# A conv and low-rank mixer on one core: earlier loads of two batches, a held transpose, and copies in one go

## The chip, the cores and the metric

The kernel runs on one core of a Trainium2 chip. The metric is the device time of one execution in microseconds; the time of a kernel is the median of several runs.

## The reference

Two layers follow one another. The first is a causal convolution over 7 taps, with one set of softmax weights for each of 8 heads of 24 channels. The second mixes along the sequence with a low-rank product, adds that to its input, and applies a two-layer network over channels, again with a residual.

```python
# x: (8, 4224, 192), weight: (8, 7); U: (4224, 32), V: (32, 4224), w_ch1: (192, 768), w_ch2: (768, 192)
w = softmax(weight, axis=-1)
y[b, s, head h] = sum over k of w[h, k] * x_padded[b, s + k, head h]   # 6 zeros ahead of x
xt = y.transpose(0, 2, 1)
h = xt @ U @ V
u = y + h.transpose(0, 2, 1)
ch = np.maximum(u @ w_ch1, 0.0) @ w_ch2
out = (u + ch).astype(np.float32)
```

## The kernel before

The 8 x 4224 rows are 264 tiles of 128 rows, 33 in a batch, and 8 tiles make a group: 33 groups in all, numbered 0 to 32. Groups are not aligned with batches: batch 0 is groups 0 to 3 and the first tile of group 4, and so on.

What is done for a batch:

- x is loaded from DRAM in four pieces (`x_part`, L76, by POOL's DMA queue, cast to bf16 on the way; the list of pieces is `XP`, L84). Pieces 0 and 1 go to the lower 64 partitions, 2 and 3 to the upper. Each batch has a tile of a pool of two (`xs`), so batch 2 takes over the memory of batch 0, and batch 3 that of batch 1. `x_zero` clears the 64 rows ahead of a batch.
- The convolution is a matmul with band matrices. Batches 0 and 1 use `conv` (L351), which reads x as loaded. Batches 2 to 7 use `conv32` (L317), which reads x and a copy shifted by 32 rows (`xb_sb`, one buffer) as well. POOL makes the copy in six steps (`x_shift`, L282, returns them as a list): two whole parts (L289, 2.74 us each, and L291, 0.50), then four that copy 32 partitions (L301, 2.74 or 3.08 us each). The result, `y_sb`, is evicted from PSUM by ACT and DVE.
- `tt` is the product with U: 33 matmuls (`tt_mm`, L391), a split into two bf16 halves (`tt_split`, L407), and a sum over four row blocks (`tt_sum`, L420: two matmuls at L423, then a cast by DVE at L417 to `tt_sb`).

What is done for a group:

- h: `h_group` (L483) multiplies `tt_sb` by V (8 matmuls at L452), and DVE adds the result to y (L474), which makes u. `transp` (L491) then has SP issue a DMA transpose of u into `uT`. Groups 0 and 1 are transposed on PE instead.
- W1: `w1` (L537), 36 matmuls at L549, with ReLU by ACT (L563) or DVE (L565). It returns the last matmul of each of its six column blocks (`ends`).
- W2: `w2` (L570), two tiles at a time: 12 matmuls at L576, an addition of u by DVE (L584), and a store that SP issues (L592).

Every engine runs its instructions in the order of the program, which is written out by hand. SP has the transposes and the stores in one row; POOL has the loads of x and the copies in one row. The order after the start is in `SLOTS` (L605). A slot names groups for W1, groups for W2, and work to be put ahead of a given pair of W2, each word a letter and numbers: `h4` is h of group 4 with its transpose, `t2` and `s2` are tt and its sum for batch 2, `c2:0:3` is conv of 3 heads of batch 2 from head 0, `d1` is conv of batch 1, `x2:4` asks for the copies of batch 2 and issues the first four steps. The steps left over are issued one after each load of the next batch, or after the W1 of a following slot.

Loads of later batches are placed by `LOADS` (L655). For each piece it names a group and a column block of its W1, and `held` (L594) makes the load wait until the last matmul of that block has run. Batch 2 has its two first pieces held to the end of W1 of group 1, and the other two to blocks 2 and 5 of W1 of group 2. The main loop (L769) goes through the slots: W1 first with the loads, then W2 pair by pair.

Of the kernel before, what the change touches and what calls it, by code (L numbers as in the profile page):

```python
# [14 lines left out]
def kernel(  # L15
# [10 lines left out]
    nc = tc.nc  # L26
# [29 lines left out]
    def bank():  # L56
        return psp.tile([P, 512], F32, name="ps", tag="ps")
# [12 lines left out]
    def x_tile(b):  # L70
        xt[b] = xs.tile([P, NB1 + 1, D], BF16, name="x_sb")

    def x_zero(b, eng):
        eng.memzero(xt[b][0:HB, 0, :])

    def x_part(b, r, s0, s1):  # L76

        blk = NB0 * r + s0 - 1
        return nc.gpsimd.dma_start(  # L79
            out=xt[b][HB * r : HB * r + HB, s0:s1, :],  # L80
            in_=x[b, blk * HB : (blk + s1 - s0) * HB, :].rearrange("(j p) d -> p j d", p=HB),
        )

    XP = [(0, 1, 17), (0, 17, NB0 + 1), (1, 0, 18), (1, 18, NB1 + 1)]  # L84
# [171 lines left out]
    def u_layout(up):  # L256
        nb = [nfull + (1 if 32 * jj < nlast else 0) for jj in range(4)]
        for a in range(4):
            for jj in range(4):
                nc.tensor.matmul(  # L260
                    out=up[jj][:, 0 : nb[jj] * R],
                    lhsT=Eq[32 * jj : 32 * jj + 32, a, :],
                    rhs=Ur[32 * jj : 32 * jj + 32, 0 : nb[jj], a * R : (a + 1) * R],
                    start=(a == 0),
                    stop=(a == 3),
                    tile_position=(32 * jj, 0),
                )
        for jj in range(4):
            evac(
                "AD"[jj % 2],  # L270
                U_sb[:, 0 : nb[jj], jj, :],
                up[jj][:, 0 : nb[jj] * R].rearrange("p (k r) -> p k r", r=R),
            )
# [77 lines left out]
    def conv(b, h0, nh, rs, engs, k0=0, k1=NT, pp=None):  # L351

        if yt[b] is None:
            yt[b] = ys.tile([P, NT, D], BF16, name="y_sb")
        nk = {r: min(k1, (NB0, NB1)[r] // 2) - k0 for r in rs}
        if pp is None:
            pp = {r: bank() for r in rs}
        w = nh * GS
        for hh in range(nh):
            h = h0 + hh  # L360
            for halo in range(2):
                for r in rs:
                    for c in range(2):
                        st = 1 - halo + c + 2 * k0
                        nc.tensor.matmul(  # L365
                            out=pp[r][HB * c : HB * c + HB, 0 : nk[r] * w].rearrange(
                                "p (k a) -> p k a", a=w
                            )[:, :, hh * GS : hh * GS + GS],
                            lhsT=bands[h // HQ][
                                HB * r : HB * r + HB, h % HQ, HB * halo : HB * halo + HB  # L370
                            ],
                            rhs=xt[b][
                                HB * r : HB * r + HB,
                                st : st + 2 * nk[r] - 1 : 2,
                                h * GS : h * GS + GS,
                            ],
                            start=(halo == 0),
                            stop=(halo == 1),
                            tile_position=(HB * r, HB * c),
                        )  # L380
        for n, r in enumerate(rs):
            j0 = NB0 // 2 * r + k0
            evac(
                engs[n % len(engs)],
                yt[b][:, j0 : j0 + nk[r], h0 * GS : h0 * GS + w],
                pp[r][:, 0 : nk[r] * w].rearrange("p (k a) -> p k a", a=w),
            )

    ttb = [[] for _ in range(B)]

# [99 lines left out]

    def transp(g):  # L491
        uTt[g] = uts.tile([P, 4, 3, P], BF16, name="uT")
        nc.sync.dma_start_transpose(
            out=uTt[g][:].rearrange("p i c t -> p (i c) t"),
            in_=ut[g][:].rearrange("p i c f k -> p (i c f k)"),
        )
# [70 lines left out]

    out_t = out.rearrange("b s d -> (b s) d").rearrange("(t p) d -> p t d", p=P)

    def w2(g, t0, n):  # L570

        hf, i = t0 // 4, t0 % 4
        cps = bank()
        for a in range(n):
            for m in range(MC):
                nc.tensor.matmul(  # L576
                    out=cps[:, a * D : (a + 1) * D],
                    lhsT=rlt[g][:, m, hf, (i + a) * P : (i + a + 1) * P],
                    rhs=W2_sb[:, m, :],
                    start=(m == 0),  # L580
                    stop=(m == MC - 1),
                )
        o = outs.tile([P, 2, D], F32, name="out_sb")
        nc.vector.tensor_tensor(  # L584
            out=o[:, 0:n, :].rearrange("p n (c k) -> p n c k", c=3),
            in0=cps[:, 0 : n * D].rearrange("p (n c k) -> p n c k", n=n, c=3),
            in1=ut[g][:, i : i + n, :, hf, :],
            op=ALU.add,
        )
        t = g * GT + t0  # L590
        eng = nc.scalar if t + n == NTT else nc.sync
        eng.dma_start(out=out_t[:, t : t + n, :], in_=o[:, 0:n, :])  # L592

    def held(ins, after):  # L594
        tc.add_manual_dep(
            ins.ins,
            after.ins.name,
            mybir.DependencyInfo(mybir.DependencyClass.Sync, mybir.DependencyReason.DATA),
            reason="load held back",
        )  # L600

    SLOTS = [  # L605
        ([0], [], {}),
        ([1], [0], {0: ["h0"], 1: ["h3"]}),
        ([2], [1], {0: ["d1", "h1"], 1: ["t1"], 3: ["s1"], 4: ["h4", "x2:4"]}),
        ([3], [2], {1: ["h5"], 3: ["h6"]}),
        (  # L610
            [4, 5],
# [2 lines left out]
                0: ["h7"],  # L614
                2: ["c2:0:3:AAD"],
                3: ["c2:3:3:AAD"],
                4: ["c2:6:2:A", "x3:3"],
                6: ["t2"],
                8: ["s2", "h8"],
                10: ["h9"],  # L620
            },
        ),
    ]
# [1 line left out]
    for k in range(5, 14):  # L625
# [13 lines left out]
        elif k < 10:  # L639
            b = k - 2  # L640
# [11 lines left out]
        SLOTS.append((gs, gs, {p: [w for w in what if w] for p, what in at.items()}))  # L652
    assert nh == NG

    LOADS = {2: [(1, 5), (1, 5), (2, 2), (2, 5)], 3: [(4, 1), (4, 4), (5, 1), (5, 4)]}  # L655
    for b in range(4, B):
        g = 3 * b - 6
        LOADS[b] = [(g, 0), (g, 3), (g + 1, 0), (g + 1, 3)]

# [21 lines left out]
        conv(0, h, 2, [0, 1], "AA" if h == 0 else "AD", *KP[0][1:])  # L681
    work = [bank() for _ in range(4)]
    u_layout(work)
    o = 0
    for js in late:
        nc.gpsimd.tensor_copy(
# [42 lines left out]
    yT_part(1, parts1)  # L729
    hT_part(1, parts1)  # L730
    band2 = cst.tile([P, H, QB], BF16, name="band2")
    x_tile(1)
    x_zero(1, nc.gpsimd)
    for xp in XP:
        x_part(1, *xp)
    for r in range(4):
        q = slice(QB * r, QB * r + QB)
# [6 lines left out]
    def do(what):  # L744
        if what[0] == "c":
            b, h0, n, engs = what[1:].split(":")
            conv32(int(b), int(h0), int(n), engs)
            return
        if what[0] == "d":
            for h in range(H):  # L750
                conv(int(what[1:]), h, 1, [0, 1], "AD")
            return
        if what[0] == "x":
            b, n = (int(v) for v in what[1:].split(":"))
            steps.extend(x_shift(b))
            for _ in range(n):
                steps.pop(0)()
            return
        n = int(what[1:])
        if what[0] == "h":  # L760
            h_group(n)
            if n > 1:
                transp(n)
        elif what[0] == "t":
            tt_split(n, tt_mm(n, range(NT)))
        else:
            tt_sum(n)

    for gs1, gs2, at in SLOTS:  # L769
        for g in gs1:  # L770
            ends = w1(g, RELU0 if g == 1 else RELU)
            for b, blocks in LOADS.items():
                for q, (gb, m) in enumerate(blocks):
                    if gb == g:
                        if q == 0:
                            x_tile(b)
                            x_zero(b, nc.gpsimd)
                        held(x_part(b, *XP[q]), ends[m])
                        if steps:
                            steps.pop(0)()  # L780
            if g == 0:
                do("h2")
        while steps and gs1 != [3]:
            steps.pop(0)()
        npc = 4 * len(gs2)
        for p in range(npc + 1):
            for what in at.get(p, []):
                do(what)
            if p < npc:
                g, k = gs2[p // 4], p % 4  # L790
                if g == NG - 1 and k == 3:
                    w2(g, 6, 1)
                    w2(g, 7, 1)
                else:
                    w2(g, 2 * k, 2)
# [30 lines left out]
```

## Time and profile before

| what | value |
|---|---|
| median of 5 runs | 328.16 us (327.48 to 328.97) |
| the profiled execution | 329.81 us |
| its span, from first to last instruction | 328.0 us |
| PE busy | 319.6 us, 97% |
| DVE busy | 270.0 us, 82% |
| ACT busy | 170.1 us, 52% |
| POOL busy | 143.6 us, 44% |
| moved by DMA | 53.52 MB, mean 163 GB/s |
| median from issue to landing: transposes of u | 4.4 us |
| the same, pieces of x (384 KB) | 8.7 us |

The engines are PE (matmuls, with PEld loading weights beside it), DVE, ACT, POOL and SP. Times are microseconds from the start of the span unless they are marked otherwise. A line of the timeline has the start, the length, the engine, the line of code, the operation, the tile written and the tile read, and a count; in brackets at its end stands how long the engine was idle before it and what ended that. The chain of waits follows the work that ended last back from the end of the span, at each step to what released it. Queue q0 of the DMA is POOL's, with the loads; q1 is SP's, with transposes and stores. The ends of matmuls are modelled, so two rows of PE may overlap. The DMA bytes of a load of x count what is written (bf16).

### The profile page before, as it was taken

Reading aid. Unit: us, or ns where it says so; the run is one execution under the profiler, and the core shown is the slowest. Engines: PE = TensorE matmul, PEld = TensorE weight load, DVE = VectorE, ACT = ScalarE, POOL = GpSimd, SP = SyncE. Lnnn points to the kernel's source line nnn. Section 1 sums busy time; section 2 is a strip of 40 time slices with the busy share of each in tenths; the row PEclk is TensorE's granted clock in tenths of the full one; section 3 lists DMA queues with packets and bytes.
Section 4 is the critical chain, followed back from the end, with each engine's and each line's share of the span. In section 5 each row is a group of like instructions: output and inputs, shape, how many; then the busy total and the mean of one; then the engine's idle time right before and its main releaser. Section 6 shows DMA issues by size and latency. Waiting matters only on the chain.

```text
span 328.0 us, 9592 instructions
## 1 busy us (share of the span) xinstructions
PE 319.6 (97%) x3998; PEld 221.5 (68%) x3998; DVE 270.0 (82%) x552; ACT 170.1 (52%) x343; POOL 143.6 (44%) x112
## 2 busy tenths in 40 slices
PE   8999999999999999999999999999999999999994
PEld 3666576577557746866874784587797497497494
DVE  7659999987877987898798799879888898896853
ACT  1667524761666198068429708834903903903900
POOL 8493229834993895967669498000000000000000
PEclk9999999999999999999999999999999999999999
DMA  9999994999999999699989967039269069049034
GB/s 105 193 132 185 200 241 111 126 192 218 252 154 185 197 188 187 180 173 168 193 236 126 221 175 195 27 107 249 59 169 265 3 153 282 2 142 244 2 129 161
DMA packets 122907, 53.52 MB, mean 163 GB/s; under 512 B 87760, under 2 KB 122832, under 8 KB 122864
## 3 DMA queue, kind: packets, MB, share of 16 engines
q1 hardware_dynamic: 84528, 38.08, 49.0%
q0 software_dynamic: 38192, 14.73, 40.3%
q8 instruction: 31, 0.51, 0.6%
q14 instruction: 12, 0.10, 0.1%
q10 hardware_dynamic: 144, 0.10, 0.1%
HBM read 29.49 MB, written 25.95 MB: 169 GB/s over the span
## 4 chain that ended last, share of the span: by engine, by line
PE 81%; POOL 8%; DMA 6%; DVE 3%; issue 1%; POOLq 0%
PE ps L576 36%; PE ps L549 32%; POOL xb_sb L301 5%; DMA x_sb<-in_x_dram 4%; PE ps L335 3%; PE ps L155 3%; PE ps L452 3%; DMA uT<-u_sb 2%; PE ps L397 2%; POOL x_sb L79 1%; PE ps L365 1%; DVE rl_sb L565 1%; DVE y_sb L254 1%; POOL xb_sb L289 1%; DVE u_sb L474 1%
## 5 line engine op out<-in xcount | busy, mean ns | idle before, releaser
L563 ACT ACTIVATE rl_sb<-ps 128x512 bf16<-128x512 f32 x233 | 124.3, 604 | 109.6 <-PE ps L549 89.3
L576 PE MATMUL ps<-W_sb,rl_sb 128*128 128x192 bf16 x1584 | 141.9, 246 | 0.2
L576 PEld LDWEIGHTS <-rl_sb 128*128 128x128 bf16 x1584 | 128.0, 98 | 13.8 <-issue 13.2
L549 PE MATMUL ps<-uT,W_sb 64*128 64x512 bf16 x1188 | 131.6, 376 | 0.6 <-DMA uT<-u_sb 0.5
L565 DVE TENSOR_SCALAR rl_sb<-ps 128x512 bf16<-128x512 f32 x163 | 105.6, 687 | 16.6 <-PE ps L549 16.4
L549 PEld LDWEIGHTS <-W_sb 64*128 64x128 bf16 x1188 | 64.0, 94 | 63.8 <-issue 3.5
L584 DVE TENSOR_TENSOR out_sb<-ps,u_sb 128x384 f32<-128x384 f32 (+1 forms) x133 | 70.3, 548 | 25.9 <-PE ps L576 25.3
L301 POOL COPY xb_sb<-x_sb 32x3072 bf16<-32x3072 bf16 (+1 forms) x24 | 67.6, 2824 | 0.7
L474 DVE TENSOR_TENSOR u_sb<-y_sb,ps 128x192 bf16<-128x192 bf16 (+1 forms) x168 | 66.2, 459 | 0.0
L289 POOL COPY xb_sb<-x_sb 128x3072 bf16<-128x3072 bf16 x12 | 32.8, 2742 | 33.5 <-DMA x_sb<-in_x_dram 21.6
L252 ACT ACTIVATE y_sb<-ps 128x408 bf16<-128x408 f32 (+4 forms) x89 | 37.8, 513 | 11.1 <-PE ps L335 8.6
L79 POOL DMA_DIRECT2D x_sb<-in_x_dram x32 | 27.0, 852 | 20.6 <-PE ps L549 13.9
L254 DVE CAST y_sb<-ps 128x408 bf16<-128x408 f32 (+4 forms) x37 | 19.7, 576 | 1.6 <-PE ps L335 0.8
L452 PE MATMUL ps<-tt_sb,V_sb 32*128 32x192 bf16 x264 | 12.6, 246 | 0.8 <-DVE tt_sb L417 0.6
L335 PE MATMUL ps<-xb_sb,band 64*32 64x384 bf16 (+1 forms) x192 | 12.4, 332 | 0.5 <-POOL xb_sb L301 0.5
L335 PE MATMUL ps<-x_sb,band 64*32 64x384 bf16 x192 | 12.1, 333 | 0.0
L452 PEld LDWEIGHTS <-V_sb 32*128 32x128 bf16 x264 | 4.7, 92 | 8.2 <-issue 8.2
L155 PE MATMUL ps<-zz 128*128 128x512 f32 x12 | 8.5, 861 | 1.5 <-DVE zz L145 1.5
L411 ACT ACTIVATE tt_hi<-ps 128x192 bf16<-128x192 f32 x8 | 2.6, 330 | 11.2 <-PE ps L397 11.1
L365 PE MATMUL ps<-x_sb,band 64*64 64x240 bf16 (+3 forms) x192 | 8.0, 276 | 0.4 <-DVE band L254 0.4
L335 PEld LDWEIGHTS <-band 64*32 64x32 bf16 x384 | 4.6, 89 | 4.9 <-issue 3.8
L365 PEld LDWEIGHTS <-band 64*64 64x64 bf16 x192 | 6.0, 106 | 2.2 <-issue 1.2
(65 smaller groups left out, 73.1 us busy)
## 6 DMA issues: line engine op xcount, KB each, us to landing
out_dram<-out_sb SPq DMA_DIRECT2D x131, 192.0 KB, 3.2
x_sb<-in_x_dram POOLq DMA_DIRECT2D x14, 384.0 KB, 8.7
x_sb<-in_x_dram POOLq DMA_DIRECT2D x7, 432.0 KB, 8.9
x_sb<-in_x_dram POOLq DMA_DIRECT2D x7, 408.0 KB, 8.5
x_sb<-in_x_dram POOLq DMA_DIRECT2D x1, 504.0 KB, 7.5
uT<-u_sb SPq DMA_TRANSPOSE x31, 4.4
x_sb<-in_x_dram POOLq DMA_DIRECT2D x1, 480.0 KB, 5.8
W_sb<-in_moe_w_ch_dram POOLq DMA_DIRECT2D x2, 192.0 KB, 7.8
```

Source lines behind the costliest of these rows:

```text
L79: return nc.gpsimd.dma_start(out=xt[b][HB * r : HB * r + HB, s0:s1, :], in_=x[b, blk * HB : (blk + s1 - s0) * HB, :].rearrange("(j p) d -> ...
L252: nc.scalar.activation(out=out, in_=in_, func=ACT.Copy)
L289: nc.gpsimd.tensor_copy(out=xbt[b][:, s0:s1, :], in_=xt[b][:, s0 + 1 : s1 + 1, :])
L301: nc.gpsimd.tensor_copy(out=xbt[b][q, s0:s1, :], in_=xt[b][q, s0:s1, :])
L335: nc.tensor.matmul(out=pp[r][QB * cg : QB * cg + QB, 0 : nk[r] * GS], lhsT=w[hr], rhs=t[hr, st : st + 2 * nk[r] - 1 : 2, hs], start=True, ...
L452: nc.tensor.matmul(out=banks[pr][:, a * D : (a + 1) * D], lhsT=V_sb[32 * q : 32 * q + 32, (j // 8) * 2 + j % 2, :], rhs=ttb[b][32 * q : 32 ...
L474: nc.vector.tensor_tensor(out=u_group(g)[:, i : i + n, :, hf, :], in0=yt[b][:, run[0] : run[0] + n, :].rearrange("p n (c k) -> p n c k", c=3),
L549: last = nc.tensor.matmul(out=pps[m][hf][:], lhsT=W1_sb[HB * hf : HB * hf + HB, c, m * P : (m + 1) * P], rhs=uTt[g][HB * hf : HB * hf + HB ...
L563: nc.scalar.activation(out=rl[:, m, hf, :], in_=pp[hf][:], func=ACT.Relu)
L565: nc.vector.tensor_scalar_max(out=rl[:, m, hf, :], in0=pp[hf][:], scalar1=0.0)
L576: nc.tensor.matmul(out=cps[:, a * D : (a + 1) * D], lhsT=rlt[g][:, m, hf, (i + a) * P : (i + a + 1) * P], rhs=W2_sb[:, m, :], start=(m == ...
L584: nc.vector.tensor_tensor(out=o[:, 0:n, :].rearrange("p n (c k) -> p n c k", c=3), in0=cps[:, 0 : n * D].rearrange("p (n c k) -> p n c k", ...
```

## The change

It has these parts:

- The tile of batch 1 is taken, its zeros written and its piece 0 loaded right after `u_layout`, ahead of POOL's copies into `U4_sb` and the loads of V and W2. Pieces 1 to 3 stay where all four were.
- Batch 2 leaves `LOADS`. The words `l2:0` to `l2:3` stand in slot 1, two ahead of the third pair of W2 of group 0 and two ahead of the fourth. Each is held to the last matmul of the pair of W2 that was issued before it (`done_w2`).
- The transpose of group 3 is no longer issued with `h3`, but after the conv of batch 1 in the program, and it is held until the last matmul of that conv. On SP it so moves past the stores of group 0.
- `x2:6` issues all six copies of batch 2 together, so that none is left over between the loads of batch 3; `x3:4` issues four copies of batch 3 together instead of three.
- In the fifth slot, `h8` moves from pair 8, where it followed `s2`, to pair 9, and `h9` from pair 10 to pair 11.

```diff
@@ in conv @@
-                        nc.tensor.matmul(
+                        last = nc.tensor.matmul(
...
+        return last
@@ in transp @@
-        nc.sync.dma_start_transpose(
+        return nc.sync.dma_start_transpose(
...
+    done_w2 = []
+
     def w2(g, t0, n):
...
-                nc.tensor.matmul(
+                last = nc.tensor.matmul(
...
+        done_w2.append(last)
         o = outs.tile([P, 2, D], F32, name="out_sb")
...
+    def x_load(b, q, after):
+        if q == 0:
+            x_tile(b)
+            x_zero(b, nc.gpsimd)
+        held(x_part(b, *XP[q]), after)
...
         ([0], [], {}),
-        ([1], [0], {0: ["h0"], 1: ["h3"]}),
-        ([2], [1], {0: ["d1", "h1"], 1: ["t1"], 3: ["s1"], 4: ["h4", "x2:4"]}),
+        ([1], [0], {0: ["h0"], 1: ["h3"], 2: ["l2:0", "l2:1"], 3: ["l2:2", "l2:3"]}),
+        ([2], [1], {0: ["d1", "h1"], 1: ["t1"], 3: ["s1"], 4: ["h4", "x2:6"]}),
         ([3], [2], {1: ["h5"], 3: ["h6"]}),
...
-                4: ["c2:6:2:A", "x3:3"],
+                4: ["c2:6:2:A", "x3:4"],
                 6: ["t2"],
-                8: ["s2", "h8"],
-                10: ["h9"],
+                8: ["s2"],
+                9: ["h8"],
+                11: ["h9"],
...
-    LOADS = {2: [(1, 5), (1, 5), (2, 2), (2, 5)], 3: [(4, 1), (4, 4), (5, 1), (5, 4)]}
+    LOADS = {3: [(4, 1), (4, 4), (5, 1), (5, 4)]}
...
     u_layout(work)
+    x_tile(1)
+    x_zero(1, nc.gpsimd)
+    x_part(1, *XP[0])
...
-    x_tile(1)
-    x_zero(1, nc.gpsimd)
-    for xp in XP:
+    for xp in XP[1:]:
         x_part(1, *xp)
@@ in do @@
         if what[0] == "d":
             for h in range(H):
-                conv(int(what[1:]), h, 1, [0, 1], "AD")
+                last = conv(int(what[1:]), h, 1, [0, 1], "AD")
+            held(transp(3), last)
+            return
+        if what[0] == "l":
+            b, q = (int(v) for v in what[1:].split(":"))
+            x_load(b, q, done_w2[-1])
             return
...
             h_group(n)
-            if n > 1:
+            if n > 1 and n != 3:
                 transp(n)
@@ in the main loop @@
-                        if q == 0:
-                            x_tile(b)
-                            x_zero(b, nc.gpsimd)
-                        held(x_part(b, *XP[q]), ends[m])
+                        x_load(b, q, ends[m])
```

More of the change, by code (lines that the diff above doesn't have):

```diff
@@ L598, in held @@
             mybir.DependencyInfo(mybir.DependencyClass.Sync, mybir.DependencyReason.DATA),
-            reason="load held back",
+            reason="transfer held back",
         )
+    def x_load(b, q, after):
[3 more added lines that the diff above has]
+        held(x_part(b, *XP[q]), after)
     SLOTS = [
         ([0], [], {}),
-        ([1], [0], {0: ["h0"], 1: ["h3"]}),
-        ([2], [1], {0: ["d1", "h1"], 1: ["t1"], 3: ["s1"], 4: ["h4", "x2:4"]}),
+        ([1], [0], {0: ["h0"], 1: ["h3"], 2: ["l2:0", "l2:1"], 3: ["l2:2", "l2:3"]}),
+        ([2], [1], {0: ["d1", "h1"], 1: ["t1"], 3: ["s1"], 4: ["h4", "x2:6"]}),
         ([3], [2], {1: ["h5"], 3: ["h6"]}),
```

## The prediction

> **What bounds the kernel now.** I read the page first, then the waits of PE, PE's timeline, the chain of waits, the DMA answers by window, and POOL's timeline. The page says that PE sets the time:
>
> ```profile
> PE 319.6 (97%) x3998; PEld 221.5 (68%) x3998; DVE 270.0 (82%) x552; ACT 170.1 (52%) x343; POOL 143.6 (44%) x112
> ...
> PE   8999999999999999999999999999999999999994
> ```
>
> PE is idle for 8.4 us in all, and its clock is full in every slice. A change that leaves PE's work alone, as this one does, can only win or lose in PE's gaps. The waits of PE name them (total, times, longest, in us):
>
> ```profile
> PE ps L155 <- DVE zz L145: 1.5, 1, 1.5
> PE ps L452 <- DVE tt_sb L417: 0.6, 1, 0.6
> PE ps L335 <- POOL xb_sb L301: 0.5, 1, 0.5
> PE ps L549 <- DMA uT<-u_sb: 0.5, 1, 0.5
> ```
>
> The first is the start. The other three lie in the part of the program that the diff touches. Where they lie is in PE's timeline (start, us, engine, line; in brackets the idle time before and who ended it):
>
> ```profile
> 35.18 4.06 PE L549 MATMUL ps<-uT,W_sb 64*128 64x512 bf16 x36 [0.51 <-DMA uT<-u_sb]
> ...
> 77.66 0.25 PE L423 MATMUL ps<-tt_hi,R 128*128 128x192 bf16 x1
> ...
> 78.74 0.34 PE L452 MATMUL ps<-tt_sb,V_sb 32*128 32x192 bf16 x6 [0.56 <-DVE tt_sb L417]
> 79.02 2.15 PE L576 MATMUL ps<-W_sb,rl_sb 128*128 128x192 bf16 x24
> ...
> 97.31 0.33 PE L335 MATMUL ps<-xb_sb,band 64*32 64x384 bf16 x1
> 98.16 0.33 PE L335 MATMUL ps<-xb_sb,band 64*32 64x408 bf16 x1 [0.51 <-POOL xb_sb L301]
> ```
>
> Idle time understates such a gap, since matmul ends are modelled; the chain of waits gives the same work undisturbed:
>
> ```profile
> 95.03 3.09 POOL xb_sb L301
> ...
> 107.63 0.17 PE ps L423 x2
> 107.80 0.28 PE ps L452 x8
> ...
> 125.72 0.64 PE ps L335 x19
> ```
>
> So the sum and h8 take 79.02 - 77.66 = 1.36 us where 0.17 + 0.28 = 0.45 would do: 0.91 lost. The first third of the conv of batch 3 takes 1.49 us (97.31 to 98.80, where the next W2 starts) against 0.64: 0.85 lost, and the last copy of batch 3, which begins at 95.03, ends it. At 35.18 the loss is 0.51. Together 2.27 us.
>
> [...] So a held load stops all that is behind it on POOL. The trace agrees: POOL stood 4.21, 5.85 and 1.60 us ahead of the held loads of batch 2. [...] The transpose of group 2 was issued at 27.99; from 29 to 31.4 the DMA answer has packets of q0, the loads, and none of q1:
>
> ```profile
> q0 software_dynamic: 1216, 0.46, 160.2%
> ...
> uT<-u_sb SPq DMA_TRANSPOSE x1, 7.1
> ```
>
> I go by the trace: a transpose waits for the loads queued ahead of it. It takes 3.2 us to land when nothing is queued (issues at 51.09 and 57.01), 7.1 and 7.0 at 27.99 and 34.76.
>
> **The change part by part.** *Batch 1 sooner.* Its zeroing (0.2) and first load (0.8 of POOL) move ahead of the U4 copies, where POOL idles 2.64 us before 14.75: free on POOL. On the DMA queue the piece (384 KB, 0.39 MB at the 192 GB/s of the answer from 29 to 31.4: 2.05 us) goes behind W1 and ahead of V and W2. The last V load lands at 18.6 + 3.8 = 22.4, and h2 needs it at 25.28: with 2.05 more, 24.5, covered by 0.8; if that cover fails, the price is what is missing of it, at most some 1 us. What is left of the backlog, W2 and batch 1, drained at about 31.8; now at 29.8. The transpose of group 2 follows: 29.8 + 3.2 = 33.0, where PE ends W2 of group 0 at 34.67. The 0.51 goes; next late is that W2 itself.
>
> *Batch 2 in W2 of group 0.* The four loads left at 30.13 (two), 37.63 and 40.07, and the first copy started at 46.85:
>
> ```profile
> 37.63 0.85 POOL L79 DMA_DIRECT2D x_sb<-in_x_dram  x1 [5.85 <-PE ps L549]
> 40.07 0.89 POOL L79 DMA_DIRECT2D x_sb<-in_x_dram  x1 [1.60 <-PE ps L365]
> 46.85 5.42 POOL L289 COPY xb_sb<-x_sb 128x3072 bf16<-128x3072 bf16 x2 [5.89 <-DMA x_sb<-in_x_dram]
> ```
>
> Now two are held to the second pair of W2 (ends near 32.6) and two to the third (33.7): issues of 0.85 each from 32.7 to 36.1. Data comes some 1.7 us later, from 34.4. They are 1.65 MB at 192 GB/s, 8.6 us, and share the engines with four stores of group 0 (0.79 MB at the 350 GB/s or so of stores alone: 2.2). They drain near 45.2, against a last landing at 40.07 + 8.9 = 49.0.
>
> *The transpose of group 3 held.* On SP it moves past the four stores of group 0 and waits for the last conv matmul of batch 1: 42.54 by PE's timeline, 42.04 after the gain above. Behind it on SP stand the stores of group 1, the first ready at 46.24, and then the transpose of group 4: nobody waits for SP. It must outlast the loads: 45.2 + 3.2 = 48.4 if it pays the whole of 3.2 after them, less as part of that is issue. PE wants it for W1 of group 3 at 48.77 - 0.51 = 48.26. That W1 takes 4.40 us against 4.06 for its neighbours, so a start up to 0.34 late may cost nothing. The bounds: below, zero (no gain is possible, the transpose was there long before); above, a landing of 11.1, the longest seen: 53.1, 4.9 us. I take 0.3.
>
> *Copies of batch 2 in one go.* Pieces 0 and 2 land near 44, so POOL's 2 x 2.74 + 0.50 + 3 x 2.74 + 3.08 = 17.3 us run 44 to 61.3 (before: to 67.2; PE comes at 68.0). The loads of batch 3 are now behind all of it: 61.5, 62.3, 63.4, 65.3 instead of 59.80, 63.35, 67.16, 68.0. The first is later, the last, which counts, 2.7 sooner: drained by 75 or so instead of 80.6 (68.0 + 12.6). Then batch 3: copies from 73, four of six steps to 84.5, a load, a copy, a load, a copy, to 92.2; PE wants them at 97.31 - 1.42 = 95.9. The 0.85 goes with 3.7 us to spare. Later batches hang on their own W1 as before and stay.
>
> *h8 and h9 one pair later.* One W2 pair (1.04 us) now covers the cast of tt_sb, so 0.91 goes. The transpose of group 8 leaves SP some 0.5 us later (80.90 + 6.5 + 0.5 = 87.9; W1 of group 8 is due at 91.3), that of group 9 1 us later and is not needed before 112. The adds of h9 on DVE come closer to W1; later slots have them there already, and their W1 takes 11.76. Free.
>
> The sum: -0.51 - 0.91 - 0.85 + 0.3 = -1.97 us. The profiled execution took 329.81 us with a span of 328.0; it would take 327.84 and 326.1. Its overhead beside the span (1.8) is untouched, so I subtract the same from the median: 328.16 - 1.97 = 326.2.
>
> **The rivals.** *Slower: the held transpose becomes the bound.* Place: W1 of group 3. Allowed landing time is 48.26 - 42.04 = 6.2 us, plus 0.34 of slack; all gains are eaten at 6.5 + 2.27 = 8.8 us, and from 9.8 the kernel is measurably slower. Of the first eleven transposes two took longer (10.2 at 59.91, 11.1 at 68.99), both issued beside loads of x, as this one is. At 10.7 the stall is 4.2: 328.16 - 2.27 + 4.2 = 330.1. Against it: at 42 all four loads were issued 6 us ago and none follows. *Little changes: the loads of batch 3 are held by the DMA engines, not by their issue.* From 63.3 to 65 next to nothing moved (0 to 5 GB/s in the DMA answer from 60 to 70) while a transpose and a load were both under way. If they still land at 80.6, four steps, then the two loads and copies end at 97.1, 1.2 after PE comes: -0.51 - 0.91 - 0.85 + 1.2 = -1.07, 327.1. For it: that stall. Against: the transpose of group 6 now leaves some 2 us before the first load. *The change doesn't do what it says* for batch 1: V, late by over 0.8, delays h2, and the 0.51 turns over: 327.2.
>
> **How the numbers follow.** Forecast 0.60 (325.5 to 327.0: all gains and the W1 slack at the low end, a transpose late by 1.1 at the high end); loads of batch 3 or V 0.22 (327.1 to 327.2, at the bound of 0.3%, 327.18; I count all but 0.02 of it as within 0.3%, since either stall is a least one); slower 0.18, two in eleven. 0.3%, some 1 us, is about what a measurement of this kernel can tell from no change. The range reaches from 325.5 to 329.0, up to the edge of the slower case, and leaves most of that out. Faster 0.62, same 0.20, slower 0.18.
>
> **What would show it.** In the trace after: no idle before L549 near 34.7, the sum followed by W2 and not by h8, no wait for xb_sb in batch 3, loads of batch 2 landed by 46, the transpose of group 3 by 48.5. Wrong if PE waits for uT before W1 of group 3 by over a microsecond, or if a new gap opens at h2.

## The result, and the profile after

| | before | after |
|---|---|---|
| median of the runs (number) | 328.62 us (79) | 330.35 us (44) |
| lowest and highest | 327.32 and 333.33 | 328.26 and 331.76 |
| the profiled execution | 329.81 us | 331.76 us |
| its span | 328.0 us | 330.0 us |
| mean granted clock of its span | 1.000 | 0.992 |

The ratio of after to before is 1.005, with a 95% interval of 1.004 to 1.0061: slower by half a per cent, where 326.2 us and a gain were forecast. (The ratio of each experiment is taken on one chip; where a ratio differs from the quotient of the medians, runs over 1.5% above the fastest of their kernel were left out of it.) The profiled run of after is the slowest of its 44, so its losses are rather large samples.

The waits of PE in the profile after (total, times, longest, in us) have one new entry, and it stands first:

```profile
PE ps L550 <- DMA uT<-u_sb: 2.4, 1, 2.4
PE ps L155 <- DVE zz L145: 1.5, 1, 1.5
```

The waits for tt_sb and for xb_sb are gone. PE's timeline of after shows where the new wait lies. L549 of before is now L550, L576 is L579, and L452 is L453:

```profile
34.63 4.06 PE L550 MATMUL ps<-uT,W_sb 64*128 64x512 bf16 x36
...
47.87 0.42 PE L453 MATMUL ps<-tt_sb,V_sb 32*128 32x192 bf16 x8
50.71 5.75 PE L550 MATMUL ps<-uT,W_sb 64*128 64x512 bf16 x36 [2.42 <-DMA uT<-u_sb]
56.39 1.17 PE L579 MATMUL ps<-W_sb,rl_sb 128*128 128x192 bf16 x12
```

W1 of group 2 (34.63) starts with no wait, 0.55 earlier than before. W1 of group 3, which followed h of group 4 directly in before, now starts 2.84 us after that h does (47.87), and then it takes 5.75 us where before it took 4.40. The windows of the same stretch show why it is long (in each row: PE, PEld, DVE, ACT and POOL busy, then the granted clock, the DMA share and GB/s):

```profile
50.00:51.00 1.00, 0.29 (x4) 0.17 (x6) 0.51 (x2) 0.00 (x0) 1.00 (x1) 1.00 1.15 367
51.00:52.00 1.00, 1.00 (x12) 0.37 (x10) 0.40 (x1) 0.39 (x1) 1.00 (x1) 0.81 1.06 350
52.00:53.00 1.00, 1.00 (x8) 0.43 (x6) 0.62 (x2) 0.58 (x2) 0.94 (x2) 0.50 2.26 188
...
54.00:55.00 1.00, 1.00 (x8) 0.36 (x6) 0.00 (x0) 1.00 (x2) 1.00 (x1) 0.50 0.89 201
55.00:56.00 1.00, 1.00 (x12) 0.49 (x10) 0.78 (x2) 0.75 (x2) 1.00 (x2) 0.98 0.00 0
```

PE is busy all the time, but runs 8 matmuls in a microsecond and not 12: about a microsecond after it came back from its idle time, the clock fell to half for some 3 us. It is no feature of this one execution. In 28 of the 44 runs of after the mean clock of the span is 0.995 or lower; of the 180 runs of before that were timed beside the experiments, this holds for 11.

The cause of the wait is in two timelines. The one of SP has the issue of the transpose (the length is that of the issue):

```profile
42.02 2.76 SPq L494 DMA_TRANSPOSE uT<-u_sb  x1
```

The one of POOL has the loads of batch 2 and the first copies made from them:

```profile
33.01 3.37 POOL L79 DMA_DIRECT2D x_sb<-in_x_dram  x4 [7.33 <-PE ps L579]
46.59 2.74 POOL L289 COPY xb_sb<-x_sb 128x3072 bf16<-128x3072 bf16 x1 [10.21 <-DMA x_sb<-in_x_dram]
49.80 2.74 POOL L289 COPY xb_sb<-x_sb 128x3072 bf16<-128x3072 bf16 x1 [0.46 <-DMA x_sb<-in_x_dram]
```

The transpose of group 3 leaves at 42.02, as predicted, and the four loads leave from 33.01. But POOL's second copy waits for a load until 49.80: so the loads drain near there and not at 45.2. The transpose lands 0.9 us later. The chain of waits has it, 8.65 us long, straight ahead of W1:

```profile
42.02 8.65 DMA uT<-u_sb
50.66 0.05 issue
50.71 5.75 PE ps L550 x36
```

**A yardstick.** Profiled runs differ at both ends for reasons that have nothing to do with the change (the last section has them). So each span is cut into three: up to the first W1 (at 21.29 in before, 21.32 in after), from there to the start of the last W1 (at 299.80 and 301.41), and the tail. The middle is 299.80 - 21.29 = 278.51 us in before and 280.09 in after. In four kernels whose PE has no wait above 0.3 us there (e9, e11, e13, e14) it repeats to a few hundredths, as the next table shows.

### The profile page after: what moved, and what is told of

Read it like the earlier page. It is cut to its first block, busy times and chain, and to the rows that moved or that the text cites. A ratio compares the mean times of both kernels' runs of the same rounds, so it can differ in the third digit from the quotient of the medians.

```text
span 330.0 us, 9589 instructions
## 1 busy us (share of the span) xinstructions
PE 320.5 (97%) x3998; PEld 223.1 (68%) x3998; DVE 269.8 (82%) x552; ACT 170.4 (52%) x343; POOL 143.7 (44%) x112
## 4 chain that ended last, share of the span: by engine, by line
PE 91%; DVE 3%; DMA 3%; ACT 1%; issue 0%
PE ps L579 40%; PE ps L550 38%; PE ps L335 3%; PE ps L453 3%; DMA uT<-u_sb 3%; PE ps L155 3%; PE ps L398 2%; DVE rl_sb L566 1%; PE ps L365 1%; ACT rl_sb L564 1%; DVE y_sb L254 1%; DVE u_sb L475 1%; PE ps L520 0%; PE ps L505 0%; DVE band L254 0%; PE ps L678 0%
## 5 line engine op out<-in xcount | busy, mean ns | idle before, releaser
L579 PE MATMUL ps<-W_sb,rl_sb 128*128 128x192 bf16 x1584 | 141.9, 246 | 0.1
L579 PEld LDWEIGHTS <-rl_sb 128*128 128x128 bf16 x1584 | 128.0, 98 | 13.5 <-issue 13.0
L550 PE MATMUL ps<-uT,W_sb 64*128 64x512 bf16 x1188 | 133.1, 380 | 2.5 <-DMA uT<-u_sb 2.4
L550 PEld LDWEIGHTS <-W_sb 64*128 64x128 bf16 x1188 | 65.8, 95 | 65.5 <-issue 5.4
L301 POOL COPY xb_sb<-x_sb 32x3072 bf16<-32x3072 bf16 (+1 forms) x24 | 67.5, 2824 | 0.7
L453 PE MATMUL ps<-tt_sb,V_sb 32*128 32x192 bf16 x264 | 12.4, 246 | 0.2 <-DVE y_sb L254 0.2
L335 PE MATMUL ps<-xb_sb,band 64*32 64x384 bf16 x192 | 12.1, 332 | 0.0
L155 PE MATMUL ps<-zz 128*128 128x512 f32 x12 | 8.5, 863 | 1.5 <-DVE zz L145 1.5
L453 PEld LDWEIGHTS <-V_sb 32*128 32x128 bf16 x264 | 4.7, 92 | 7.5 <-issue 7.5
```

The lines of the kernel that those rows point to most:

```text
L301: nc.gpsimd.tensor_copy(out=xbt[b][q, s0:s1, :], in_=xt[b][q, s0:s1, :])
L335: nc.tensor.matmul(out=pp[r][QB * cg : QB * cg + QB, 0 : nk[r] * GS], lhsT=w[hr], rhs=t[hr, st : st + 2 * nk[r] - 1 : 2, hs], start=True, ...
L453: nc.tensor.matmul(out=banks[pr][:, a * D : (a + 1) * D], lhsT=V_sb[32 * q : 32 * q + 32, (j // 8) * 2 + j % 2, :], rhs=ttb[b][32 * q : 32 ...
L550: last = nc.tensor.matmul(out=pps[m][hf][:], lhsT=W1_sb[HB * hf : HB * hf + HB, c, m * P : (m + 1) * P], rhs=uTt[g][HB * hf : HB * hf + HB ...
L579: last = nc.tensor.matmul(out=cps[:, a * D : (a + 1) * D], lhsT=rlt[g][:, m, hf, (i + a) * P : (i + a + 1) * P], rhs=W2_sb[:, m, :], start ...
```

## The experiments

Ratios of experiments are to before on the same chip, where before's own median was 328.30 to 328.62 us; middle and tail are of each kernel's one profiled run, worked out as above.

| label | kernel | median us (runs) | ratio (interval) | middle us | tail us |
|---|---|---|---|---|---|
| | before | 328.62 (79) | 1 | 278.51 | 28.20 |
| | after | 330.35 (44) | 1.005 (1.004 to 1.0061) | 280.09 | 28.59 |
| e1 | after, no hold | 338.49 (6) | 1.0202 (1.0161 to 1.0243) | 290.73 | 28.29 |
| e2 | before, hold | 328.91 (22) | 1.0016 (0.9995 to 1.0037) | 277.64 | 28.24 |
| e3 | before, h8 and h9 later | 329.02 (22) | 1.0009 (0.9992 to 1.0027) | 281.06 | 28.05 |
| e4 | after, PE kept busy | 330.20 (12) | 1.0051 (1.0034 to 1.0068) | 280.14 | 28.29 |
| e5 | before, batch 1 sooner | 327.53 (22) | 0.9971 (0.9954 to 0.9987) | 276.82 | 28.06 |
| e6 | e3, ten output buffers | 327.38 (22) | 0.9962 (0.9948 to 0.9977) | 278.22 | 27.31 |
| e7 | before, ten output buffers | 327.64 (22) | 0.997 (0.9952 to 0.9988) | 277.81 | 27.52 |
| e8 | after, loads of batch 2 last | 344.0 (1) | none | 293.65 | 28.00 |
| e9 | after, old loads of batch 2 | 328.55 (14) | 1.0001 (0.998 to 1.0023) | 276.14 | 28.23 |
| e10 | after, ten output buffers | 329.46 (22) | 1.0034 (1.002 to 1.0049) | 280.10 | 27.30 |
| e11 | before, batch 1 sooner, h8 and h9 later, ten buffers | 326.32 (7) | 0.994 (0.9919 to 0.9961) | 276.17 | 27.42 |
| e12 | e9, ten output buffers | 327.35 (22) | 0.9958 (0.9941 to 0.9976) | 278.06 | 27.49 |
| e13 | e11, copies in one go | 325.79 (6) | 0.9924 (0.9904 to 0.9944) | 276.16 | 27.52 |
| e14 | e11, hold | 326.72 (15) | 0.9948 (0.9932 to 0.9963) | 276.17 | 27.44 |

My theory after the result was that the transpose of group 3 lands late because of the loads queued ahead of it. The rivals were that the hold itself makes it late, that the clock and not the wait is the loss, and that something else (h8 and h9) takes the gains back.

**e1: after without the hold.**

```diff
-            held(transp(3), last)
...
-            if n > 1 and n != 3:
+            if n > 1:
```

> The changed kernel, but the transpose of group 3 is issued with h3 as before and not held. Theory A (the held transpose lands too late behind the loads of batch 2, so that PE waits 2.4 us before W1 of group 3 and then runs that W1 at a lower clock; the other parts give their 2.3 us): no wait for uT there, W1 of group 3 back to 4.1 to 4.4 us, clock 1.0, and some 2 us faster than before (about 326.5, ratio 0.993 to 0.995). Theory B (the early loads of batch 2 jam the DMA engines, whether the transpose is held or not): the transpose, issued at about 34.8 behind two to four of these loads, still lands after 48, and the time stays near 330, ratio 1.003 or more.

This fits neither theory whole: W1 of group 3 starts on time (47.99, 4.41 us), as A had it, but the kernel is slower than B's 330 us, the slowest of all but e8. The profile is of the slowest of its six runs (341.89 us; the fastest took 333.01), so its losses are large samples. In it the transpose, issued at 34.55 amid the loads, needs 12.3 us, and the last load of batch 2 is seen by POOL only at 52.94. So the copies end at 67.5, and all four loads of batch 3 leave together at 67.72, beside the transpose of group 7 (68.21, which takes 11.0). POOL's timeline of e1:

```profile
67.72 3.37 POOL L79 DMA_DIRECT2D x_sb<-in_x_dram  x4
87.45 2.74 POOL L289 COPY xb_sb<-x_sb 128x3072 bf16<-128x3072 bf16 x1 [16.35 <-DMA x_sb<-in_x_dram]
```

PE then waits 8.9 us in all for xb_sb in the conv of batch 3. Next to early loads the hold is a help (a ratio of 1.005 against 1.0202). In this profile a transpose among loads delays the loads, too (POOL saw the last of batch 2 at 52.94, in after at 49.80), and the price is paid a batch later.

**e2: before with the hold alone.** The conv returns its last matmul, and the transpose of group 3 is held to it, as in the change:

```diff
+            held(transp(3), last)
...
-            if n > 1:
+            if n > 1 and n != 3:
```

> The kernel before with only the hold of the transpose of group 3. Theory A: it stands behind the last two loads of batch 2, issued 2 to 5 us ahead of it; they drain near 45, the transpose lands at 47.5 to 49 where PE comes at 48.8, so the wait is 0 to 0.5 us, and batch 2 and 3 arrive sooner: ratio 0.996 to 1.002. If the hold costs by itself whatever stands in the queue: PE waits 2 us or more before W1 of group 3, ratio 1.007 or more.

W1 of group 3 starts at 49.24 without a wait and takes 4.40. With the loads of before, a held transpose of group 3 is in time.

**e8: after with the loads of batch 2 behind that transpose.**

```diff
-        ([1], [0], {0: ["h0"], 1: ["h3"], 2: ["l2:0", "l2:1"], 3: ["l2:2", "l2:3"]}),
+        ([1], [0], {0: ["h0"], 1: ["h3"]}),
-        ([2], [1], {0: ["d1", "h1"], 1: ["t1"], 3: ["s1"], 4: ["h4", "x2:6"]}),
+        ([2], [1], {0: ["d1", "h1"], 1: ["t1"], 2: ["l2:0", "l2:1", "l2:2", "l2:3"], 3: ["s1"], 4: ["h4", "x2:6"]}),
```

> The changed kernel with the four loads of batch 2 held to the second W2 pair of group 1 (issued near 46.7), so that none is ahead of the transpose of group 3. Theory A (that transpose was late because of the loads queued ahead of it): it is issued at 42.0 and lands by 46, and PE does not wait before W1 of group 3. If the hold to the conv is to blame whatever is queued: it lands at 48 or later. The loads are too late for the conv of batch 2 here, so PE is expected to wait some 5 to 9 us for xb_sb near 68, and the total says nothing.

The transpose of group 3 landed in 3.2 us, where 8.6 were needed behind the loads, and W1 of group 3 had no wait. The next transposes now stood behind the loads: they took 11.4, 10.4 and 7.9 us, and W1 of groups 4 and 5 had the same fate, in PE's timeline of e8:

```profile
47.46 4.40 PE L550 MATMUL ps<-uT,W_sb 64*128 64x512 bf16 x36
...
61.18 10.88 PE L550 MATMUL ps<-uT,W_sb 64*128 64x512 bf16 x72 [4.45 <-DMA uT<-u_sb]
```

(72 matmuls take 8.24 us in before.) So the backlog of loads makes the transpose late, and the stall goes where the loads go. (It does so in two ways that e8 doesn't part: the transpose meets the loads, and it stands on SP's queue behind stores that met them too: the three issued from 46 to 48 us took a median of 7.4 us to land.) The whole kernel is much slower (344.0 us), as batch 2 is late as well.

**e9: after with the loads of batch 2 held as before.** All other parts of the change stay.

```diff
-    LOADS = {3: [(4, 1), (4, 4), (5, 1), (5, 4)]}
+    LOADS = {2: [(1, 5), (1, 5), (2, 2), (2, 5)], 3: [(4, 1), (4, 4), (5, 1), (5, 4)]}
```

and the four words `l2` leave `SLOTS`.

> The changed kernel with the loads of batch 2 held as before (two to the end of W1 of group 1, two to blocks 2 and 5 of W1 of group 2); the hold of the transpose of group 3 and all else stay. Theory A (the four loads put together in W2 of group 0 are what the held transpose stands behind, and that is the loss): the transpose lands before PE wants it, no lower clock in W1 of group 3, and with the sooner piece of batch 1 the kernel is faster than before, ratio 0.995 to 0.999. Theory B (another part of the change costs: copies in one go, the later h9): ratio 1.002 or more.

The median falls by 330.35 - 328.55 = 1.8 us against after (1.6 by the ratios). The profile, of its fastest run, has no wait for uT, W1 of group 3 at 47.33 in 4.40 us, and a middle of 276.14. The median is no better than before, though, and its runs spread from 326.59 to 331.75; e12 to e14 take that up.

**e4: after with PE kept busy.** Three matmuls without use stand ahead of W1 of group 3, so that PE works while it waits:

```diff
+            if g == 3:
+                fill = bank()
+                for _ in range(3):
+                    nc.tensor.matmul(out=fill[:], lhsT=zz[:, 0:P], rhs=zz[:], start=True, stop=True)
```

> The changed kernel with three matmuls of zeros (0.86 us each, 2.6 in all, into a bank that nobody reads) put ahead of W1 of group 3 on PE. If the lower clock in that W1 comes from the idle time before it: PE does not idle, the clock stays at 1.0, W1 of group 3 takes 4.1 to 4.5 us instead of 5.75, and the kernel is about 1 us faster than the changed one, ratio to before 0.999 to 1.003. If the lower clock has another cause: W1 still takes over 5 us and the ratio is 1.005 or more.

PE's timeline of e4:

```profile
47.27 2.84 PE L791 MATMUL ps<-zz 128*128 128x512 f32 x6
50.05 4.06 PE L550 MATMUL ps<-uT,W_sb 64*128 64x512 bf16 x36
```

W1 is back to 4.06 us, and the clock of the whole span is 1.0; none of the 12 runs of e4 has a mean clock under 0.997. So the slow W1 of after comes from the idle time. W2 of group 3 started at 54.04 - 20.37 = 33.67 after the first W1, against 56.39 - 21.32 = 35.07 in after, so 1.4 us are won there. The expected microsecond did not come in the median, though (330.2). This profile loses the 1.4 us again: 1.0 between h8 and W1 of group 6, where DVE waits 1.9 us for a store, and 0.45 in W1 of groups 6 to 8 (12.46 us and not 12.01). Whether the other runs lose them in the same place isn't shown.

**e5: before with piece 0 of batch 1 early.** The three lines that follow `u_layout` in the change, alone.

```diff
     u_layout(work)
+    x_tile(1)
+    x_zero(1, nc.gpsimd)
+    x_part(1, *XP[0])
```

> The kernel before with only piece 0 of batch 1 loaded sooner. The prediction's step: the loads ahead of the transpose of group 2 drain 2 us sooner, so PE does not wait for uT near 35, and the 0.5 to 2.1 us seen there in the runs so far go: ratio 0.996 to 0.999. If the sooner piece only displaces V or W2: a wait at h2 or at the first W2, ratio 1.000 or more.

A gain of 328.47 - 327.53 = 0.94 us. The wait for uT ahead of W1 of group 2 is gone. In e11, which has the same lines, the transposes of groups 2 and 3 take 5.6 and 5.3 us (7.1 and 7.0 in before).

**e3: before with h8 and h9 later.**

```diff
-                8: ["s2", "h8"],
-                10: ["h9"],
+                8: ["s2"],
+                9: ["h8"],
+                11: ["h9"],
```

> The kernel before with only h8 and h9 moved one pair of W2 later. The prediction's step: the sum and h8, 1.36 us together, lose their wait, 0.9 us faster (ratio 0.997). If that wait is given back elsewhere (a W1 waiting for the later transposes or for DVE): ratio 1.000.

No gain in the median (+0.4 us; the interval includes 1). The wait for tt_sb is gone, but in the profile DVE waited 1.41 us for an output buffer whose store had not landed, right ahead of h8's adds, and W1 of groups 6 to 8 took 12.46 us where before took 11.83. It seemed that the buffers take the gain back, so two more kernels had ten of them and not eight.

**e6 and e7: ten output buffers, with h8 and h9 later and without.**

```diff
-tc.tile_pool(name="outs", bufs=8)
+tc.tile_pool(name="outs", bufs=10)
```

> The kernel before with h8 and h9 one pair later and ten buffers for the output tile instead of eight. Theory A (the gain of moving h8 was given back because DVE, ahead of the adds of h8, then waits 1.4 us for an output buffer whose store is stuck behind the loads of batch 3): with two buffers more DVE does not wait, W1 of group 6 to 8 takes 11.8 us again, not 12.46, and the ratio is 0.997 to 0.998. Theory B (it is the adds of h9 so near to W1 that cost): W1 stays at 12.4 us, ratio 1.000 or more.

> The control: the kernel before with only the ten output buffers. In the order of before the adds of h8 stand ahead of the waiting addition on DVE, whose wait is 0.3 us: ratio 0.999 to 1.001 under either theory.

e6 gains as hoped (0.9962), and in its profile DVE no longer waits for a store there and that W1 takes 11.90. But the control e7, expected at 0.999 to 1.001, gains nearly all of it alone (0.997). So most of the gain isn't the wait in the middle. The tails of the table tell where ten buffers gain: 27.30 to 27.52 us in all seven kernels with ten buffers, 28.00 to 28.59 in all nine with eight. The last two stores land sooner. The DMA view of before from 310 us on has them so (KB each, us to landing):

```profile
out_dram<-out_sb SPq DMA_DIRECT2D x1, 96.0 KB, 3.0
out_dram<-out_sb ACTq DMA_DIRECT2D x1, 96.0 KB, 2.9
```

The same of e7:

```profile
out_dram<-out_sb SPq DMA_DIRECT2D x1, 96.0 KB, 2.4
out_dram<-out_sb ACTq DMA_DIRECT2D x1, 96.0 KB, 1.9
```

My theory had the wait right and its share of the gain wrong. What h8 and h9 later are worth is 0.3 us by medians (e6 against e7, intervals overlapping) and 276.82 - 276.17 = 0.65 by the middles of e5 and e11.

**e10 and e12: ten output buffers in after, and in e9.** The edit of e7.

> The changed kernel with ten output buffers. The wait of DVE for a store ahead of the adds of h8 (0.4 to 1.9 us in the changed order) goes, the late transpose of group 3 stays: ratio to before 1.001 to 1.004, some 0.6 us under the changed kernel. If that wait is most of the loss: ratio 0.999 or less.

> The changed kernel with the loads of batch 2 held as before and ten output buffers. If the early loads were the only part that costs: at or below the run with the sooner piece of batch 1, the later h8 and ten buffers, ratio 0.992 to 0.995. If the hold or the copies in one go cost too: above that run by 0.5 us or more.

e10 has the same late transpose (a wait of 2.53 us, W1 5.75 us, middle 280.10) and is 0.9 us faster by medians, 0.5 by ratios whose intervals overlap; in the profile the tail is 1.29 us shorter and the middle the same. e12 against e10 is the early loads again: 329.46 - 327.35 = 2.1 us on one chip.

**e11: the parts that gained, on before.** The edits of e5, e3 and e7 together; no hold, no early loads of batch 2, copies as in before.

> The kernel before with the sooner piece of batch 1, h8 and h9 one pair later, and ten output buffers, loads and transposes as before. If the gains of the parts add (0.9 and 1.1 us by their own runs): ratio 0.993 to 0.995. If they share one cause, the loads' backlog: ratio 0.996 to 0.997.

326.32 us, below both kernels. Its PE has no waits but the start and 0.2 us for y_sb. It is 1 us below e12, which has the hold and the copies in one go as well; two more kernels ask which of these costs it.

**e13 and e14: e11 with the copies in one go, and with the hold.** For e13:

```diff
-        4: ["h4", "x2:4"]
+        4: ["h4", "x2:6"]
...
-        4: ["c2:6:2:A", "x3:3"]
+        4: ["c2:6:2:A", "x3:4"]
```

For e14, the edit of e2.

> The version of 326.32 us (early piece of batch 1, h8 and h9 later, ten output buffers, no hold) with only the copies in one go added (six of batch 2, four of batch 3). Theory A, the copies are what kept the version with the old loads 1 us above it: the loads of batch 3 stand behind six copies, the first of them leaves only after 64 us, the last copies of batch 3 come late, PE waits for xb_sb near 97 for about 1 us; ratio to before 0.997, near 327.3. Theory B, the copies cost nothing and the hold does: ratio 0.994, near 326.3, no wait for xb_sb.

> The same version of 326.32 us with only the hold of the transpose of group 3 added (behind the conv of batch 1). Theory A, the hold costs nothing with the old loads: W1 of group 3 starts without a wait, the transposes of groups 4 and 5 come no later, ratio 0.994, near 326.3. Theory B, the hold pushes the stores of group 1 and the transpose of group 4 back on SP and PE waits there: ratio 0.997, near 327.3. If both this and the copies give 0.994, the 1 us between the two versions was within their intervals.

Neither costs anything that shows alone: the middles are 276.16 and 276.17 against 276.17, and the three ratios overlap. e13 has the lowest median, 325.79 us or 0.9924 (0.9904 to 0.9944), and beats both kernels; its interval overlaps those of e11 and e14. The waits of PE that it has left:

```profile
PE ps L155 <- DVE zz L145: 1.5, 1, 1.5
PE ps L365 <- DVE band L254: 0.4, 1, 0.4
PE ps L452 <- DVE y_sb L254: 0.2, 1, 0.2
```

Both parts together (e12) are above e13, and the intervals just touch. In the profile of e12 the conv of batch 3 waits 1.3 us for xb_sb, and the transpose of group 7, issued next to the loads of batch 3, takes 11.9 us (9.2 in e13). That fits a chance collision which the hold makes more likely, and it would explain the spread of e9; neither was shown, and e12 and e13 ran on two chips.

## Why the prediction was wrong

**The step that failed** is the one on the held transpose: "They drain near 45.2", and from that "I take 0.3". That the loads could hold the transpose up was foreseen, and it was issued at 42.02 (42.04 predicted). Two terms of the sum were mis-sized.

- *The drain.* The sum had data from 34.4 at 192 GB/s and the stores at 350. The DMA view of after shows a mean of 165 GB/s from 36 to 40 us, when only the loads move, 239 from 40.5 to 44, when three stores of group 0 move beside them, and about 80 from 48.5 to 49.5, when the last of the loads and the transpose are under way. The last two pieces land 11.8 and 14.3 us after issue, the last of them near 49.8 and not at 45.2. The landing of the transpose came to 8.65 us where 6.2 were allowed: a wait of 2.42 against the 0.3. The picture behind the sum, a transpose that starts when the loads have drained, was wrong as well: from 46 to 48 both moved side by side (the last section has the packets).
- *The clock.* It was in no step. The rival "the held transpose becomes the bound" named the place, and from its own figures a landing of 8.65 gives a stall of 8.65 - 6.2 = 2.45, measured 2.42. But it priced the wait alone, so that its break-even lay at 8.8 us and a landing of 8.65 would still have been a net gain. In the profile a slow clock came on top: 5.75 - 4.40 = 1.35 us. With it, the break-even lies where idle time begins to cost clock, by my estimate between 1.72 and 2.06 us: of the single profiles of e6 and e3, the first has a full clock after its wait and the second one of 0.50.

So W2 of group 3 starts, in the profile, 3.28 us later than before (56.39 against 53.11), after the gain of 0.55: the term is 3.83 us, not 0.3. That is 3.5 of the 3.97 us between the forecast of -1.97 and the +2.0 of the two profiled spans.

The medians give it less. Between the forecast and the measured +1.73 lie 3.7 us, and taking the early loads out wins 1.6 to 1.8 (e9) or 2.1 (e12 against e10). So about half of the miss is the late transpose. The other half is gains that the forecast read off one profile and that the median doesn't show: e9, with every part but the early loads, is no faster than before (328.55 us against 328.41 on its chip). The clock may be a smaller part than in the profile, too: the 28 runs of after with the lower clock have a median of 330.44 us, the other 16 one of 329.68.

**The other steps.** *Batch 1 sooner* held: -0.51 predicted, -0.55 in the profile after, -0.94 in the median of e5; in the profiles of e2, e3, e6 and e7, which load batch 1 as before does, that wait was 0.74, 2.06, 1.72 and 0.92, so before's 0.51 was the smallest of five samples. *h8 and h9 later* held in part: in after the offset to before falls from 3.29 us at the sum (80.95 against 77.66) to 2.54 at W1 of group 6 (86.01 against 83.47), so 0.75 of the 0.91 came. "Free" was too much said for it: alone (e3) it gave no gain in the median.

*Conv of batch 3* came out by luck. PE had no wait there, and the offset falls from 2.72 at the end of W1 of group 8 to 1.87 after the conv (100.67 against 98.80), which is the 0.85. But the working failed. The copies of batch 2 were to run from 44 to 61.3, and those of batch 3 to end at 92.2. They ran from 46.59 to 64.38, and POOL's last copy of batch 3 in after is this:

```profile
94.90 3.08 POOL L301 COPY xb_sb<-x_sb 32x3456 bf16<-32x3456 bf16 x1
```

It ends at 97.98, just as in before (98.1). PE didn't wait because it came to that conv 2.72 us late itself. The wait was no fixed cost either: the profiles of e2, e3, e5, e6 and e7 don't have it, though they load batch 3 as before does, so the medians can hardly have held it.

The middles of the profiles agree with the sum better than the medians do. Without the late transpose the middle is 276.14 - 278.51 = -2.37 us (e9), where the prediction had -0.51 - 0.91 - 0.85 = -2.27; but before's one profile has the chance wait of 0.85 in it, and e9's profile is its fastest run. In after it is +1.58. The part between, 3.95 us, is the transpose: 2.49 of wait with its issue (50.71 against 48.22, 0.35 after the start of h4), 1.35 of clock, and 0.11 at W1 of groups 6 to 8.

**The rivals.** "The held transpose becomes the bound" was right, with a chance of 0.18 that was too low. Its evidence against itself, that "at 42 all four loads were issued 6 us ago", took issue for progress: four loads issued within 3.4 us are 1.65 MB in the queue. "Loads of batch 3 are held by the DMA engines" came true in its figures: it had them land at 80.6 and the copies end at 97.1, and in after POOL took the second load at 81.47. Whether the engines or the issue held them stays open, as the last load left at 69.15, later than the 68.0 of before. "V late" did not occur.

**What stays open.** Medians and profiles don't agree for the kernels with the hold and the old loads (e9: middle -2.37, median 0.0), so half of the miss is explained only in part, by the chance wait of before; one profile in 14 runs doesn't tell what the others waited for. Why the loads ran at 165 GB/s here and at 192 in before isn't known. Why ten buffers make the last stores land sooner wasn't tried.

## What to carry to other kernels

A transfer that PE needs at a set time shares the DMA engines with what is queued ahead of it and beside it (here a transpose landed in 3.2 us alone, in e8, and in 8.65 behind 1.65 MB of loads, in after): before loads are moved forward, count their bytes against the deadline of the next transfer that PE waits for, at the rate that loads and stores reach together (239 GB/s in after from 40.5 to 44 us), and let the forecast have a margin of microseconds, not tenths. Price a new PE wait as idle time plus the clock that it may cost, which in the profile here made 2.4 us into 3.8. Before a gap of one profile is booked as a gain, look whether other profiles have it. Compare one stretch of PE's timeline between two of its own events, and not spans, when gains of half a microsecond are at stake.

## What the runs showed of the hardware

**Idle time and the clock.** Waits of PE of 2.06 (e3) and 2.42 us (after) were each followed by a clock of 0.50 for some 3 us. With one of 4.45 us (e8) the clock was at 0.67 in the last full microsecond of the wait and at 0.50 in the six that follow. After one of 2.53 us (e10) the page has a clock of 0.7 in the slice from 49.3 to 57.5 us. 36 matmuls then took 5.75 us in e3, after and e10, 72 took 10.88 in e8. After waits of 0.92 (e7) and 1.72 us (e6) 36 matmuls took 4.06, and the windows of e6 have a clock of 1.00. Each is one profile, so between 1.72 and 2.06 us lies no more than a first guess at where the clock begins to fall. The windows of e3:

```profile
36.00:37.00 1.00, 0.97 (x8) 0.46 (x10) 0.00 (x0) 0.00 (x0) 0.00 (x0) 0.75 1.60 187
37.00:38.00 1.00, 1.00 (x8) 0.31 (x5) 0.69 (x1) 0.60 (x1) 0.00 (x0) 0.50 1.44 215
```

**Transposes beside loads.** The same transpose of 128 x 1536 took 3.2 us when nothing else was queued (e8) and 8.6, 11.4 and 12.3 us behind or among loads (after, e8, e1). The prediction read one stretch of before, where no packet of q1 moved, as a transpose that waits for the loads queued ahead of it. In the later traces there are stretches in which both queues move at the same time. The DMA view of e8 from 56 to 58 us, with two transposes (q1) and the loads (q0) under way, has packets, MB and share of the engines so:

```profile
q0 software_dynamic: 558, 0.21, 84.8%
q1 hardware_dynamic: 557, 0.14, 53.8%
```

The two queues move one for one here, and q1 gets 557 packets through in 2 us, where the transpose of group 3 alone moved 1568 in as long (42 to 44 us). In after, stores of group 0 and loads do the same from 41 to 42 (215 and 220 packets), and these stores stand ahead of the held transpose on its own queue. Then it moves beside the last loads. The view of after from 46 to 47 us:

```profile
q0 software_dynamic: 353, 0.14, 110.2%
q1 hardware_dynamic: 183, 0.05, 35.5%
```

Its issue on SP is longer, too: 2.76 us, against 1.39 in e8 with nothing queued. Why no packet of q1 moves in some stretches (from 29 to 31.4 us in before, with a transpose issued at 27.99, and from 36 to 39 in after, with stores issued by 37.4) stays open.

**Two starts.** The first W1 begins at 20.07 to 20.59 us in eight of the profiled runs and at 21.08 to 21.52 in the other eight, whatever the change. The first ten matmuls of the program (L155) take 5.97 to 6.69 us in the first eight (5.97 in e7) and 7.18 to 7.62 in the others (7.39 in before), so the difference is there by 9.1 us. With one profile of each kernel it isn't known how often each start comes, but a difference of 1 us between two spans can lie there alone.

**The last stores.** Eight or ten buffers for the output, and nothing else changed, moved the landing of the very last store from 2.9 us (before) to 1.9 (e7). It took 2.7 to 3.2 us in all nine profiles with eight buffers and 1.8 to 2.1 in all seven with ten.
